# One attention-and-gMLP kernel on one core: the first pair's work cut and zeros added at the change of lag, copies ahead of the pieces' conversions, later pieces, and two fill units moved into the scores' banks

## The chip, the cores and the metric

The kernel runs on one core of a Trainium2 chip. The metric is the device time of one execution in microseconds (us), lower is better. The engines named below are TensorE (PE, with its weight loads as PEld), VectorE (DVE), ScalarE (ACT), GpSimd (POOL) and SyncE (SP), which issues most of the DMAs.

## The reference, cut to what matters

```python
# attention: 2 batches, 12 heads, 448 positions, head size 64
scores = scale * np.matmul(q, k.transpose(0, 1, 3, 2))
scores = cap * np.tanh(scores / cap)
attn = softmax(scores)                  # with 1e-9 added to the sum
x = merge_heads(np.matmul(attn, v))     # (2, 448, 768)

# first block: gMLP, 768 -> 1024 -> 768
h = gelu_tanh(x @ w_in); u, v = halves(h)
v_n = layernorm(v) * g_ln
gated = u * (w_sg @ v_n + b_sg)
x = x + gated @ w_out

# second block: gated convolution, 768 -> 1024 -> 768
h = relu(x @ w_in2)
out = (h * sigmoid(conv3(h, conv_w))) @ w_out2
```

## The kernel before

Every large product is three passes of matmuls on numbers that are split into a high and a low part (hi*hi, hi*lo, lo*hi). The kernel has three stages on TensorE: attention, the first block (units u, v, sg and o), the second block (units h and f).

**Attention** takes the 24 heads as 12 pairs (pair N is two heads). The loop runs over rounds R: round R makes the scores of one half of the keys of pair N = R // 2, so an even round is the first half, an odd round the second. In a round TensorE makes scores (tile sc, four banks that every round uses again), ScalarE makes tanh (line 387, sc to raw) and exp (line 388, raw to raw), and TensorE multiplies raw with V into the tile pv (`sums`, three banks; two pairs in turn share the middle one). The values lag behind the scores: LAGS says one round up to round 2 and two rounds from round 3. After the second half of a pair, `norm` copies values and softmax sums out of pv into E (ScalarE, line 504), which frees the banks for the next values; `s1`, some half rounds later, takes the reciprocal of the sums ss that a DMA has brought (DVE, lines 519 and 520), `s1b` spreads it by DMA to rb, and `s2` multiplies (line 536) and splits the result into X (ACT and DVE, lines 105 and 106). The last pair goes through `norm_pe`: copy E (line 548), reciprocal on VectorE (550, 551), four matmuls with sel (line 555), product (559). VectorE also prepares Q and K of the next pair (`prep_q`, `prep_k`; kl is the last part of K) and adds the halves of raw into sm for the sums.

**Beside it** the first block's weights are brought in as 12 pieces of w_in. Each piece lands in a tile f64, its top 16 bits are turned into half floats in the tile hd (line 149 on ACT, line 151 on DVE while R < 11), then merged (line 154), and cast to the high part of WI (160) and the low part (163). WIN gives the round in which a piece's DMA is issued, `wait` how many ticks later each of the three steps is due; there are two ticks in a round. hd is one tile, so a piece's conversion waits until the one before it has been read.

**Fill units.** Units u 0 to 2 of the first block for batch 0 are made inside the attention loop, as the table FILL says: round: (unit, first k, last k). All of them use the one bank of psm (tag mo), which `u_done` frees by the gelu on ACT and DVE (lines 221, 224, 225 and 228, the last into u). Unit u 3 is the first after the loop (mo, lines 109 to 111), then come the v units (lines 724 to 726).

**Order.** The order of each engine's instructions is fixed when the program is built, by a scheduler that works with its own estimate of the times; `pin` forces an instruction behind another, `ordered` pins a matmul behind the one before it in the loop, and `later` puts a step off by ticks. The warming matmuls wps and the matmuls named idle multiply zeros (wz) and are read by nobody. SP's DMAs are in the order in which the code issues them.

## Time and profile before

| | us |
|---|---|
| runs | 333.1, 335.48, 338.03 |
| median | 335.48 |
| profiled execution | 337.11 |
| its span in the profile | 335.3 |
| busy: PE, DVE, ACT, POOL | 318.5, 238.3, 223.2, 37.6 |
| granted TensorE clock, mean | 0.985 |

The profiled execution is one execution; its time is the span plus 1.8 us around it. A timeline line has the start, the duration, the engine, the line, operation and tiles, and in square brackets how long the engine sat idle before it and who ended that wait. Matmuls are pipelined: a row of several has their first start and their last modelled end, and the next row may start before it.

### The profile page before, as it was taken

The numbers are of one execution on the slowest core, as the hardware profiler recorded it, in microseconds if no ns is written. First come the engines' busy times: TensorE is split into PE (matmuls) and PEld (weight loads), VectorE is DVE, ScalarE is ACT, GpSimd is POOL, SyncE is SP. The second block draws the span as 40 slices with busy tenths as digits, with TensorE's granted clock in tenths as the row PEclk, the third lists the DMA queues.
The fourth block names the chain that finished last, engine by engine and source line by source line (L and its number), as shares of the span: only waits on it lengthen the run. The fifth ranks groups of instructions, "written<-read, shape, count | busy, mean of one in ns | idle before, by whom it ended". The sixth has DMA issues, their size and how long they took to land.

```text
span 335.3 us, 6265 instructions
## 1 busy us (share of the span) xinstructions
PE 318.5 (95%) x2380; PEld 262.8 (78%) x2380; DVE 238.3 (71%) x471; ACT 223.2 (67%) x357; POOL 37.6 (11%) x74
## 2 busy tenths in 40 slices
PE   7979999999788999999999999999999999999992
PEld 6445666656556778988899999999999999999991
DVE  4556586585965589996998789996975999980000
ACT  2887999999896257675765565555855988873010
POOL 4000130440304320221111000000000000000000
PEclk9978999999999999999999999999999999999998
DMA  5586595778422134212323490002392123012211
GB/s 141 150 193 187 154 259 171 199 216 189 133 75 76 38 123 108 69 38 78 121 71 125 124 343 20 0 2 63 71 334 100 31 65 94 0 59 112 82 55 35
DMA packets 22062, 37.73 MB, mean 113 GB/s; under 512 B 7320, under 2 KB 14376, under 8 KB 22024
## 3 DMA queue, kind: packets, MB, share of 16 engines
q1 hardware_dynamic: 20152, 34.41, 34.3%
q0 software_dynamic: 1632, 2.61, 3.1%
q8 instruction: 20, 0.33, 0.4%
q10 hardware_dynamic: 240, 0.23, 0.3%
q14 instruction: 18, 0.15, 0.2%
HBM read 34.40 MB, written 2.79 MB: 111 GB/s over the span
## 4 chain that ended last, share of the span: by engine, by line
PE 79%; ACT 10%; DMA 4%; SPq 2%; issue 2%; DVE 1%; ACTq 0%; DVEq 0%
PE mo L109 18%; PE mo L110 18%; PE mo L111 18%; PE pv L373 8%; PE sc L373 6%; ACT raw L387 4%; PE mo L724 3%; PE mo L726 3%; PE mo L725 3%; SPq L83 2%; ACT raw L388 2%; PE mo L373 2%; DMA qr<-in_qT_dram 1%; ACT hd L149 1%; DMA f<-in_conv_w_dram 1%
## 5 line engine op out<-in xcount | busy, mean ns | idle before, releaser
L109 PE MATMUL mo<-X,WI 128*128 128x448 f32 x126 | 46.0, 367 | 0.3 <-DVE u L228 0.3
L110 PE MATMUL mo<-X,WI 128*128 128x448 f32 x126 | 46.0, 366 | 0.0
L111 PE MATMUL mo<-X,WI 128*128 128x448 f32 x126 | 45.9, 365 | 0.0
L373 PE MATMUL pv<-raw,V 128*32 128x224 f32 x576 | 34.6, 370 | 3.5 <-ACT E L504 3.3
L388 ACT ACTIVATE raw<-raw 128x1792 f32<-128x1792 f32 (+3 forms) x26 | 36.7, 1413 | 0.8
L387 ACT ACTIVATE raw<-sc 128x1792 f32<-128x1792 f32 (+1 forms) x22 | 32.4, 1472 | 5.0 <-PE sc L373 4.9
L110 PE MATMUL mo<-HG,W 128*128 128x448 f32 x96 | 34.8, 365 | 0.0
L111 PE MATMUL mo<-HG,W 128*128 128x448 f32 x96 | 34.7, 365 | 0.0
L109 PE MATMUL mo<-HG,W 128*128 128x448 f32 x96 | 34.1, 365 | 0.0
L373 PE MATMUL sc<-Q,K 64*128 64x448 f32 x216 | 29.9, 399 | 3.8 <-ACT raw L387 3.3
L373 PEld LDWEIGHTS pv<-raw,V 128*32 128x32 f32 x576 | 19.1, 112 | 16.6 <-ACT E L504 6.0
L373 PEld LDWEIGHTS sc<-Q,K 64*128 64x128 f32 x216 | 19.1, 192 | 14.7 <-ACT raw L387 8.1
L179 ACT ACTIVATE f<-f 128x256 f32<-128x256 f32 (+2 forms) x44 | 22.8, 518 | 10.2 <-DMA f<-in_w_out_dram 6.2
L189 DVE SCALAR_TENSOR_TENSOR f<-f 128x256 uint32<-128x256 uint32 (+2 forms) x44 | 22.3, 515 | 8.2 <-ACT f L182 8.0
L109 PEld LDWEIGHTS mo<-X,WI 128*128 128x128 f32 x126 | 23.6, 188 | 2.8 <-DVE u L228 0.8
L110 PEld LDWEIGHTS mo<-X,WI 128*128 128x128 f32 x126 | 23.7, 188 | 2.0
L111 PEld LDWEIGHTS mo<-X,WI 128*128 128x128 f32 x126 | 23.6, 188 | 2.0
L904 ACT ACTIVATE o<-mo 128x448 f32<-128x448 f32 x12 | 6.3, 542 | 24.7 <-PE mo L111 20.8
L182 ACT ACTIVATE f<-f 128x256 uint32<-128x256 uint32 (+2 forms) x44 | 22.7, 515 | 0.0
L192 DVE SCALAR_TENSOR_TENSOR f<-f 128x256 uint32<-128x256 uint32 (+2 forms) x44 | 22.4, 515 | 0.1
L110 PEld LDWEIGHTS mo<-HG,W 128*128 128x128 f32 x96 | 18.0, 188 | 1.4
L109 PEld LDWEIGHTS mo<-HG,W 128*128 128x128 f32 x96 | 18.0, 188 | 1.4
(148 smaller groups left out, 685.8 us busy)
## 6 DMA issues: line engine op xcount, KB each, us to landing
f<-in_w_in_dram SPq DMA_DIRECT2D x12, 512.0 KB, 4.4
f<-in_w_out_dram SPq DMA_DIRECT2D x24, 256.0 KB, 4.5
f<-in_w_in_dram SPq DMA_DIRECT2D x12, 511.8 KB, 5.1
f<-in_w_out_dram SPq DMA_DIRECT2D x8, 384.0 KB, 3.1
qr<-in_qT_dram SPq DMA_DIRECT2D x24, 112.0 KB, 3.7
out_dram<-o SPq DMA_DIRECT2D x12, 224.0 KB, 1.9
rb<-d POOLq DMA_DIRECT2D x22, 112.0 KB, 4.0
V<-in_vL_dram SPq DMA_DIRECT2D x12, 192.0 KB, 3.3
```

The costliest lines, as they stand in the source:

```text
L109: matmul(ps, lhsT=whi, rhs=xhi, start=start, stop=False)
L110: matmul(ps, lhsT=whi, rhs=xlo, start=False, stop=False)
L111: matmul(ps, lhsT=wlo, rhs=xhi, start=False, stop=stop)
L179: A.activation(f(h), f(h), AF.Copy, scale=2.0**-112)
L182: A.activation(l, l, AF.Copy, scale=0.93 * 2.0**-29)
L189: V.scalar_tensor_tensor(out=l, in0=h, scalar=3, in1=l, op0=ALU.logical_shift_left, op1=ALU.bitwise_or)
L192: V.scalar_tensor_tensor(out=l, in0=h, scalar=0x80000000, in1=l, op0=ALU.bitwise_and, op1=ALU.bitwise_or)
L373: lastm[0] = T.matmul(*args, **kw)
L387: A.activation(x, ps, AF.Tanh, **sc)
L388: lasta[0] = A.activation(x, x, AF.Exp, scale=creg)
L724: T.matmul(ps, lhsT=xs(0, k), rhs=WI[1][:, 0, k], start=k == 0, stop=False)
L725: T.matmul(ps, lhsT=xs(0, k), rhs=WI[1][:, 1, k], start=False, stop=False)
```

## The change

Eight edits, in the code of the attention and of what it shares with the slow path:

1. In `constants` the product with guard and the tile eye leave the fast path; hd becomes two tiles that pieces use in turn.
2. For pair 0, K is prepared ahead of Q, Q's high part is copied by ScalarE, and the guard's product comes behind.
3. For pair 0 the order on ScalarE is tanh, tanh, exp, exp for round 0 and one tanh and one exp for round 1; the values of round 0 come after all scores of round 1.
4. Zero matmuls: 4 in round 0 as before, 2 in round 1, and 9 behind the scores of round 3.
5. The copy E of pair 0 comes behind the tanh of round 3. The tanh and exp instructions are pinned in order.
6. The columns (gbc and conv_w) are loaded in round 6 instead of round 1.
7. Pieces are issued later (WIN), their steps come one tick later (`wait`), and the steps of `norm` come two and one ticks later for pairs below 8.
8. Unit u 1 is made in round 24 instead of 23, and units u 1 and u 2 go to banks of the tile fi, which is the scores' tile sc, instead of psm's bank.

```diff
-FILL = {14: (0, 0, 2), 18: (0, 2, 4), 22: (0, 4, 6), 23: (1, 0, 6), 25: (2, 0, 6)}
+FILL = {14: (0, 0, 2), 18: (0, 2, 4), 22: (0, 4, 6), 24: (1, 0, 6), 25: (2, 0, 6)}
-IDLE = 4
+IDLE = {0: (0, 4), 1: (3, 2), 3: (3, 9)}
-WIN = (3, 5, 8, 10, 12, 14, 15, 17, 18, 20, 21, 22)
+WIN = (3, 5, 7, 9, 12, 15, 17, 19, 21, 22, 23, 24)
...
-        heads[:] = [pool.tile([P, 512], U32, name=f"hd{i}") for i in range(1)]
+        heads[:] = [pool.tile([P, 512], U32, name=f"hd{i}") for i in range(2)]
...
-                V.tensor_copy(q[:, 0], qr)
-                V.tensor_tensor(out=q[:, 1], in0=qr, in1=f(q[:, 0]), op=ALU.subtract)
+                A.activation(q[:, 0], qr, AF.Copy)
+                lastv[0] = V.tensor_tensor(out=q[:, 1], in0=qr, in1=f(q[:, 0]), op=ALU.subtract)
...
+        prep_k(0)
         prep_q(0)
-        prep_k(0)
+        with pin(lastv):
+            V.tensor_scalar(out=guard, in0=guard, scalar1=1e-9, scalar2=None, op0=ALU.mult)
...
             def soft(x, ps):
-                A.activation(x, ps, AF.Tanh, **sc)
-                lasta[0] = A.activation(x, x, AF.Exp, scale=creg)
+                with pin(lasta):
+                    lasta[0] = A.activation(x, ps, AF.Tanh, **sc)
+                if N == 1 and half:
+                    with pin(lasta):
+                        late.pop()()
+                if half or N:
+                    expo(x)
+
+            def expo(x):
+                with pin(lasta):
+                    lasta[0] = A.activation(x, x, AF.Exp, scale=creg)
...
+                if N == 0 and g < 2:
+                    soft(raw[:, 2 * g : 2 * g + 2], ps[:, 2 * g : 2 * g + 2, :S])
+                    if g:
+                        expo(raw[:, 0:2])
+                        expo(raw[:, 2:4])
+                if R in IDLE and g == IDLE[R][0]:
+                    for _ in range(IDLE[R][1]):
                         ordered(idle, lhsT=wz[:, :P], rhs=wz, start=True, stop=True)
...
-            A.activation(e[:, j * (S + HS) : (j + 1) * (S + HS)], both, AF.Copy)
-            u = j * (2 * S + HS)
-            G.dma_start(ss[j * P // m : (j + 1) * P // m], e[::32, u : u + HS])
+
+            def copy():
+                lasta[0] = A.activation(e[:, j * (S + HS) : (j + 1) * (S + HS)], both, AF.Copy)
+                u = j * (2 * S + HS)
+                G.dma_start(ss[j * P // m : (j + 1) * P // m], e[::32, u : u + HS])
+
+            if N:
+                copy()
+            else:
+                late.append(copy)
...
-            later(4, s1)
-            later(5, s1b)
-            later(13, s2)
+            k = 6 if N < 8 else 4
+            later(k, s1)
+            later(k + 1, s1b)
+            later(14 if N < 8 else 13, s2)
...
-            if R == 1:
+            if R == 6:
                 columns(att)
...
-                    wdec(*wi_piece(w_in, j // NK, j % NK), att, 4, hi_eng="v", wait=(3, 4, 5), top_eng=top_eng)
+                    wdec(*wi_piece(w_in, j // NK, j % NK), att, 4, hi_eng="v", wait=(4, 5, 6), top_eng=top_eng)
...
                 if k0 == 0:
-                    fill[i] = psm.tile([P, 512], F32, tag="mo", name="mo")[:, :S]
+                    if i == 1:
+                        fill[3] = psa.tile([P, 4, 512], F32, tag="sc", name="fi", bufs=1)
+                    fill[i] = fill[3][:, i, :S] if i else psm.tile([P, 512], F32, tag="mo", name="mo")[:, :S]
```

The scheduler then puts the instructions in this order. TensorE in the first pair, from its first scores to the first matmul of round 4, before:

```order
L373 MATMUL sc<-Q,K_87 128x448 x6
L373 MATMUL idle<-wz 128x448 x4
L373 MATMUL sc<-Q,K_87 128x448 x6
L373 MATMUL pv<-raw,V 32x224 x8
L373 MATMUL sc<-Q,K_87 128x2x224 x6
L373 MATMUL pv<-raw,V 32x224 x8
L373 MATMUL sc<-qr,kl_91 64x224 x4
L373 MATMUL pv<-sm,ones_152 32x224 x4
...
L373 MATMUL sc<-Q,K_88 128x2x224 x6
L373 MATMUL sc<-qr,kl_92 64x224 x4
L373 MATMUL sc<-Q,K_87 128x448 x12
```

TensorE at the same place after the change:

```order
L377 MATMUL sc<-Q,K_87 128x448 x6
L377 MATMUL idle<-wz 128x448 x4
L377 MATMUL sc<-Q,K_87 128x448 x6
L377 MATMUL sc<-Q,K_87 128x2x224 x6
L377 MATMUL sc<-qr,kl_91 64x224 x4
L377 MATMUL idle<-wz 128x448 x2
L377 MATMUL pv<-raw,V 32x224 x16
L377 MATMUL pv<-sm,ones_148 32x224 x4
...
L377 MATMUL sc<-qr,kl_92 64x224 x4
L377 MATMUL idle<-wz 128x448 x9
L377 MATMUL sc<-Q,K_87 128x448 x12
```

The values of round 0 moved behind the scores of round 1, and nine zero matmuls stand between the scores of round 3 and those of round 4.

ScalarE from the tanh of round 16 to that of round 20, before (E is the copy out of pv, X the attention's result, hd a piece's conversion):

```order
L387 ACTIVATE raw_938<-sc_937 128x1792
L388 ACTIVATE raw_938<-raw_938 128x1792
L105 ACTIVATE X_75<-E_513 128x2x448
L149 ACTIVATE hd0_141<-f64_884 128x512
L387 ACTIVATE raw_995<-sc_994 128x1344
L388 ACTIVATE raw_995<-raw_995 128x1344
L504 ACTIVATE E_920<-pv_171 128x672
L387 ACTIVATE raw_1045<-sc_1044 128x1792
L388 ACTIVATE raw_1045<-raw_1045 128x1792
L149 ACTIVATE hd0_141<-f64_992 128x512
L387 ACTIVATE raw_1096<-sc_1095 128x1344
```

ScalarE at the same place after the change:

```order
L394 ACTIVATE raw_937<-sc_936 128x1792
L403 ACTIVATE raw_937<-raw_937 128x1792
L105 ACTIVATE X_75<-E_518 128x2x448
L394 ACTIVATE raw_990<-sc_989 128x1344
L403 ACTIVATE raw_990<-raw_990 128x1344
L149 ACTIVATE hd0_140<-f64_887 128x512
L521 ACTIVATE E_924<-pv_168 128x672
L394 ACTIVATE raw_1042<-sc_1041 128x1792
L403 ACTIVATE raw_1042<-raw_1042 128x1792
L394 ACTIVATE raw_1095<-sc_1094 128x1344
```

One conversion of two is gone from these rounds, and the other one stands later, ahead of a copy E.

TensorE from the last scores (round 23) to the first v unit, before (mo and fi are fill units, sel the norm of the last pair):

```order
L373 MATMUL sc<-qr,kl_92 64x224 x4
L373 MATMUL mo<-X,WI_76 128x448 x18
L373 MATMUL pv<-raw,vlast 64x224 x4
...
L373 MATMUL pv<-raw,V 32x224 x16
L373 MATMUL pv<-sm,ones_152 32x224 x4
L373 MATMUL mo<-X,WI_76 128x448 x18
L373 MATMUL pv<-raw,vlast 64x224 x4
...
L109 MATMUL mo<-X,WI_76 128x448
L110 MATMUL mo<-X,WI_76 128x448
...
L555 MATMUL pv<-E,sel 64x224 x4
L724 MATMUL mo<-WI_77,X 128x512
```

TensorE at the same place after the change:

```order
L377 MATMUL sc<-qr,kl_92 64x224 x4
L377 MATMUL pv<-raw,vlast 64x224 x4
...
L109 MATMUL mo<-X,WI_76 128x448
L110 MATMUL mo<-X,WI_76 128x448
L377 MATMUL fi<-X,WI_76 128x448 x18
...
L377 MATMUL pv<-raw,V 32x224 x16
L377 MATMUL pv<-sm,ones_148 32x224 x4
...
L377 MATMUL fi<-X,WI_76 128x448 x18
L377 MATMUL pv<-raw,vlast 64x224 x4
...
L578 MATMUL pv<-E,sel 64x224 x4
L752 MATMUL mo<-WI_77,X 128x512
```

The fourth unit u (lines 109 to 111, 18 matmuls) moved from behind the last values to ahead of the last fill unit; the matmuls with sel now come directly behind the last values.

VectorE after the change, from the gelu of the last fill unit to the reciprocal that those matmuls wait for:

```order
L224 SCALAR_TENSOR_TENSOR g0_1412<-g0_1412,fi_1338 128x448
L228 SCALAR_TENSOR_TENSOR u_1455<-g0_1412,fi_1338 128x448
L558 TENSOR_TENSOR E_1129<-E_1129,rb_1232 128x896
L154 SCALAR_TENSOR_TENSOR f64_1336<-f64_1336,hd0_140 128x512
L573 TENSOR_SCALAR E_1438<-E_1438,one_72 128x224
L160 CAST WI1_77<-f64_1336 128x512
L574 RECIPROCAL E_1438<-E_1438 128x224
```

Before, the same row stood without the two steps of a piece (lines 154 and 160).

## Rows read from the trace of the kernel before

**Rows 1.** Stretches: start:end, length, busy of each engine, PEclk, DMA share, GB/s.
```profile
121.00:300.00 179.00, 179.00 (x868) 162.20 (x865) 160.95 (x318) 123.77 (x260) 10.58 (x14) 1.00 0.28 88
```

**Rows 2.** Timeline, rounds 0 to 2.
```profile
7.17 0.97 PE L373 MATMUL sc<-Q,K 64*128 64x448 f32 x6 [0.41 <-DVE one L258]
8.19 1.01 ACT L387 ACTIVATE raw<-sc,one 128x896 f32<-128x896 f32 x1 [2.58 <-PE sc L373]
9.23 0.95 ACT L388 ACTIVATE raw<-raw 128x896 f32<-128x896 f32 x1
16.38 0.23 ACT L149 ACTIVATE hd<-f 128x24 f16<-128x24 bf16 x1 [1.11 <-DMA f<-in_conv_w_dram]
17.00 1.65 ACT L387 ACTIVATE raw<-sc 128x1792 f32<-128x1792 f32 x1
```

**Rows 3.** Timeline, rounds 3 to 6, around the change of lag.
```profile
20.29 0.71 ACT L504 ACTIVATE E<-pv 128x672 f32<-128x672 f32 x1
20.90 1.28 ACT L387 ACTIVATE raw<-sc 128x1344 f32<-128x1344 f32 x1
22.24 2.61 PE L373 MATMUL sc<-Q,K 64*128 64x448 f32 x12 [2.11 <-ACT raw L387]
24.89 1.67 ACT L387 ACTIVATE raw<-sc 128x1792 f32<-128x1792 f32 x1 [1.35 <-PE sc L373]
31.98 1.49 PE L373 MATMUL sc<-Q,K 64*128 64x448 f32 x12
```

**Rows 4.** Stretches of TensorE's waits and of the work behind one.
```profile
20.13:22.24 2.11, 0.00 (x1) 0.01 (x2) 1.82 (x4) 2.08 (x4) 0.68 (x1) 0.85 0.86 239
22.24:28.30 6.06, 6.06 (x52) 3.73 (x52) 3.31 (x7) 4.66 (x3) 0.00 (x0) 0.50 1.12 227
...
85.85:87.64 1.79, 0.00 (x1) 0.00 (x1) 1.79 (x6) 1.41 (x3) 0.00 (x0) 1.00 0.75 233
```

**Rows 5.** Timeline, rounds 8 to 10.
```profile
39.51 0.71 ACT L504 ACTIVATE E<-pv 128x672 f32<-128x672 f32 x1
...
40.28 1.76 PE L373 MATMUL pv<-raw,V 128*32 128x224 f32 x32
...
45.74 1.49 PE L373 MATMUL sc<-Q,K 64*128 64x448 f32 x12
```

**Rows 6.** Timeline, TensorE's waits in rounds 16 to 20, and what leads to the last.
```profile
69.98 1.76 PE L373 MATMUL pv<-raw,V 128*32 128x224 f32 x32 [0.55 <-ACT E L504]
...
76.05 1.49 PE L373 MATMUL sc<-Q,K 64*128 64x448 f32 x12 [0.54 <-ACT raw L387]
...
84.15 0.23 DVE L519 TENSOR_SCALAR ss<-ss,one 128x14 f32<-128x14 f32 x1 [4.29 <-DMA ss<-E]
85.52 0.68 DVE L154 SCALAR_TENSOR_TENSOR f<-f,hd 128x512 uint32<-128x512 uint32 x1
86.23 0.78 ACT L149 ACTIVATE hd<-f 128x512 f16<-128x512 bf16 x1 [1.13 <-DMA V<-in_vL_dram]
87.64 1.76 PE L373 MATMUL pv<-raw,V 128*32 128x224 f32 x32 [1.79 <-ACT E L504]
```

**Rows 7.** Timeline, from the last scores to the norm of the last pair.
```profile
100.77 3.94 PE L373 MATMUL mo<-X,WI 128*128 128x448 f32 x18 [1.36 <-DVE u L228]
107.90 1.76 PE L373 MATMUL pv<-raw,V 128*32 128x224 f32 x32 [0.97 <-ACT E L504]
108.90 0.45 DVE L160 CAST WI<-f 128x512 fp32r<-128x512 f32 x1
109.97 3.94 PE L373 MATMUL mo<-X,WI 128*128 128x448 f32 x18
116.47 0.47 PE L109 MATMUL mo<-X,WI 128*128 128x448 f32 x1 [0.34 <-DVE u L228]
117.70 1.55 DVE L551 RECIPROCAL E<-E 128x224 f32<-128x224 f32 x1
120.34 0.98 PE L555 MATMUL pv<-E,sel 128*64 128x224 f32 x8
```

More of the change, by code (lines that the diff above doesn't have):

```diff
@@ L257, in constants @@
         A.activation(guard, ncap, AF.Exp)
-        V.tensor_scalar(out=guard, in0=guard, scalar1=1e-9, scalar2=None, op0=ALU.mult)
-        heads[:] = [pool.tile([P, 512], U32, name=f"hd{i}") for i in range(1)]
+        if not bounded:
+            V.tensor_scalar(out=guard, in0=guard, scalar1=1e-9, scalar2=None, op0=ALU.mult)
+        heads[:] = [pool.tile([P, 512], U32, name=f"hd{i}") for i in range(2)]
         for t in heads:
             G.memset(f(t), 0.0)
-        eye = pool.tile([P, P], F32, name="eye")
-        make_identity(nc, eye)
         G.memset(nhalf, -0.5)
-        return eye
+        if not bounded:
+            eye = pool.tile([P, P], F32, name="eye")
+            make_identity(nc, eye)
+            return eye
     def columns(pool):
@@ L362, in attention @@
             G.memset(sel[t * 32 : t * 32 + 1, t], 1.0)
+        prep_k(0)
         prep_q(0)
-        prep_k(0)
+        with pin(lastv):
+            V.tensor_scalar(out=guard, in0=guard, scalar1=1e-9, scalar2=None, op0=ALU.mult)
         raws, acc, held, pairs = {}, {}, {}, []
@@ L373, in ordered @@
                 lastm[0] = T.matmul(*args, **kw)
+        late, sm0 = [], [None]
         sums = psa.tile([P, 3 * 512], F32, tag="pv", name="pv", bufs=1)
         def scores(N, half, ahead={}):
+            R = 2 * N + half
             q, K = Qt[N], Kt[N % 2]
@@ L419, in scores @@
                             )
[L420 to L433 removed]
+                if N == 0 and g < 2:
[5 more added lines that the diff above has]
+                    for _ in range(IDLE[R][1]):
+                        ordered(idle, lhsT=wz[:, :P], rhs=wz, start=True, stop=True)
+            if half:
+                soft(raw, ps)
+            elif N:
+                soft(raw, ps[:, :, :S])
             if half == 0:
                 held[N] = att.tile([P, 2, S], F32, tag="sm", name="sm", bufs=2)
[L436 removed]
+                sm = V.tensor_tensor(out=held[N], in0=raw[:, 0:2], in1=raw[:, 2:4], op=ALU.add)
+                if N == 0:
+                    sm0[0] = sm
         def start_values(N):
@@ L582, in attention @@
                     start_values(0)
-                    scores(N, half, {2: lambda: value(0, 0), 3: lambda: value(0, 1)})
+                    scores(N, half)
+                    value(0, 0)
+                    value(0, 1)
                     values(0, 0, True)
@@ L588, in attention @@
                 if half == 0 and N + 1 < NN:
-                    prep_q(N + 1)
-                    prep_k(N + 1)
+                    with pin(sm0) if N == 1 else ExitStack():
+                        prep_q(N + 1)
+                        prep_k(N + 1)
             if R in FILL:
```

14 lines of the change are left out of this document (removed).

## The prediction

> **What bounds the kernel now.** I read the busy times by stretch first. From 121 to 300 us TensorE is busy all of 179.00 us at a granted clock of 1.00 [rows 1]: nothing that the change does there can bring anything, and the matmuls there are the same before and after. What can be won or lost lies in the first 121 us, so I went through the timeline of those for every place where TensorE waits, and read who ends the wait. There are four kinds.
>
> First, the first pair. ScalarE takes it in small pieces, each tanh waiting for its scores and each exp following it, then serves the two copies of the conv columns (0.23 us for the first), and starts the tanh of round 2 at 17.00 [rows 2]. Second, the change of lag at round 3. There the copy of the first sums (0.71) stands between exp and the tanh of round 3 (1.28), and the scores of round 4 wait 2.11 us for that tanh [rows 3]. This is costly twice. TensorE is idle from 20.13 to 22.24, its clock falls to 1.2 GHz inside that wait, and the next 6.06 us of work run at 0.50 [rows 4]. ScalarE itself then waits 1.35 us for the slow scores [rows 3]. Another wait, 1.79 us, at 85.85, left the clock at 1.00 [rows 4].
>
> Third, from 24 to 54 us the engines are balanced: the copy E ends at 40.22 and the matmuls that need its bank start at 40.28 [rows 5]. From round 12 on the pieces' conversions (0.78 each) and the attention's copies to X come on top on ScalarE, and TensorE waits 0.55, 0.54 and 1.79 us [rows 6]. The last of these is a chain: VectorE waits 4.29 us for the DMA of the sums ss, so the reader of hd (0.68) comes late, hd has one buffer, the next conversion waits 1.13 us, and the copy E behind it lets TensorE wait [rows 6]. Fourth, the fill units at the end share one bank: 1.36 us for the unit's result u, 0.97 for a copy E, 0.34 again for u [rows 7].
>
> **The change part by part.** Small pieces of round 0 and 1: K's high part is made first on VectorE while ScalarE makes Q's. The first scores wait 0.41 us after the warming matmuls now [rows 2]; that is all that can go, so 0 to 0.4, and I take 0.3, since the data still has to land. Then tanh, tanh, exp, exp and one tanh of 1.28 stand on ScalarE. The second tanh still cannot start before its scores, which in both programs wait for the first tanh; now that point is 10.18 (end of the first exp) [rows 2], then 9.85. From there: 1.01, twice 0.95 and 1.28 give 14.1. The scores of round 2 may start then, with some 0.4 for the sums' matmuls ahead, and take 1.49 as any such group [rows 3]: tanh of round 2 at 16.05 against 17.00, a gain of 0.95. The conv columns are away from here; on SP's queue their two DMAs now stand ahead of the loads for pair 5 instead of pair 3, which are due two rounds later.
>
> Zeros at the lag change: the copy E now comes after tanh of round 3, so that tanh starts 0.95 and 0.71 sooner than 20.90, at 19.3 at the earliest; its scores, after which TensorE falls idle at 20.13 now [rows 4], are ready at about 19.4, because the tanh of round 2 that they wait for ends sooner. It ends at 20.8. The nine zero matmuls, some 0.2 each (18 matmuls of that width take 3.94 us [rows 7]), fill TensorE from 19.4 to 21.2, so the scores of round 4 start at 21.2 at full clock and end at 22.7. ScalarE needs until 22.85 for copy and exp (about as long as its tanh). So tanh of round 4 starts at 22.85 instead of 24.89 [rows 3]. From a tanh right behind a copy (40.3) to the scores of the pair after (45.74) it takes 5.4 at full clock [rows 5], so the scores of round 6 start at 28.2 instead of 31.98: **a gain of 3.8**, 3.0 to 4.2 by the unknown landing times.
>
> Conv columns in round 6: two copies of 0.23 on ScalarE in a period that has 0.06 us to spare between E and the matmuls [rows 2, 5]: **a loss of 0.3**, 0 at least, 0.5 at most; should their DMA be late, more, but it is issued before the round that reads it.
>
> Conversions behind the copies, two hd buffers, later pieces: in the rounds up to the last tanh there were seven conversions on ScalarE, now there are four; three go to the end, where ScalarE waits anyhow. The wait for hd's reader goes, since hd has two buffers and the norm's first step comes two ticks later, when ss has landed. Of the three waits of TensorE, 2.88 us in all [rows 6], I keep 0.2 before the values of round 14, 0.1 before the scores of 18, 0.75 before the values of 18 (a conversion of 0.78 still stands ahead of the copy there) and 0.2 after a copy to X: 1.25. **A gain of 1.6**, 0.5 to 2.9.
>
> Last units in the scores' banks: now the order on TensorE decides. The three waits of [rows 7], 2.67 us, go: the values of round 21 come before the fill, and the units no longer share a bank. But the fourth unit (mo, lines L109 to L111), which before stood between the last values and the matmuls of the norm (pv from E and sel), is used up ahead. What is late next is the norm of the last pair. Before, the reciprocal ended at 119.25, that is 5.34 after the last fill ended at 113.91, hidden by the fourth unit [rows 7]. After, the same chain holds, with a piece's two steps more on VectorE in between, 0.68 and 0.45 less their overlaps [rows 6, 7]: 6.45 after the last fill. The last values take only 2.2 of that. So TensorE waits 4.2 us there, with the v units behind it. Before, the norm's matmuls started at 120.34; the stream without its waits would be there at 117.7, or at 117.0 if the drains ahead of the waits go too. So the last fill ends at 114.8 to 115.5 and these matmuls start at 121.2 to 121.9, on the time axis of the kernel before. **A loss of 1.2**, 0.9 to 1.5.
>
> And the clock. The wait of 2.11 us let it fall and the wait of 1.79 did not [rows 4]; one of 4.2 is twice the longer. I let it fall. The first 6.06 us of work after the wait at 22.24 ran at 0.50, which is worth 3.0 us of time [rows 4]: **a loss of 3.0** for the first v unit, 0 if the clock holds, 3.5 at the most.
>
> Without cost: the eye tile that is no longer made, the guard's product behind prep_q (VectorE has slack there), and GpSimd's set-up instruction, which moves to the first pow, where GpSimd waits for VectorE's statistics; the v units have banks to run ahead. The norm's first step comes two ticks later, so on GpSimd's queue a next pair's ss goes ahead of rb; rb is read rounds later. VectorE has one more piece to finish after the norm, in a stretch in which TensorE's own delay gives it the time.
>
> Sum: -3.8 + 0.3 - 1.6 + 1.2 + 3.0 = -0.9 us. Against the profiled execution (337.11, of which 335.3 are the span) that is 336.2; this execution lies 1.6 above the median of the runs, 335.48, and from that the time is **334.6**.
>
> **The rivals.** The clock holds through the wait at the norm: everything else the same, 331.6. For it speaks the wait of 1.79 without a fall, against it the one of 2.11 with one [rows 4]. The Trainium skill (TensorE: Matmul & The Clock Gate, Part 1: The HAM clock gate) calls the point at which the clock switches run-variable; by that some executions would show this time and others my forecast's, and no run here shows it either way.
>
> The conversions are not what held TensorE (or the wait for ss comes back one round later): the 1.6 stays, and the time is 336.2, no gain at all. For it: ScalarE is full there, and one conversion still stands ahead of a copy. Against: the chain in [rows 6] is closed, link by link.
>
> Slower: the zeros do not hold the clock. In the first pair the scores of round 1 must now wait for the second tanh, about 1 us (1.01 for the tanh itself [rows 2]), with shorter waits around it, where before values stood in between. If these add up as the wait of 2.11 us did, the clock falls there, 3.0 us as in [rows 4] come back at the start, and the norm's fall stays: 337.6, slower by 0.6%. It decides from the point at which the granted clock of 10 to 22 us goes to 0.50. Against it: none of these waits alone is longer than the one of 1.79.
>
> **How the numbers follow.** Forecast 0.50; clock holds 0.20; conversions without effect 0.17; clock falls at the start as well 0.13. The low end is the second case with the start's gain at its upper bound, rounded for the middle's, 330.8; the high end the last case, 337.6, and a little of its bound, 338.0. All four cases lie within 2% of 335.48 (328.8 to 342.2), about what a measurement of this kernel tells from no change: faster 0.04, same 0.93, slower 0.03.
>
> **What would show it.** Right: scores of round 6 at about 28 and a granted clock of 1.00 from 10 to 34 us; the last attention tanh about 5 us sooner; a wait of TensorE of some 4 us ahead of the norm's matmuls, ended by VectorE's reciprocal, and 0.50 behind it. Wrong: if the wait is under 2 us, my chain on VectorE is too long; if it is there and the clock stays at 1.00, the second case holds; if TensorE waits for bank or weights in the v units, the late last piece costs what I put at nothing.

## The result, and the profile after

The changed kernel is slower: 338.86 us median (336.16 to 341.64, 20 runs) against 336.08 us for the kernel before on the same chip (333.10 to 338.91, 20 runs). The ratio is 1.0091, with a 95% interval of 1.0067 to 1.0115; all ratios here are of the runs within 1.5% of their kernel's fastest, so they differ a little from those of the medians. The prediction was 334.6 us with a range of 330.8 to 338.0: the time moved the other way and ended outside the range. The profiled execution of the changed kernel took 340.46 us, of which 338.7 are the span.

The timeline of the changed kernel at its start, and around the change of lag (start us, length us, engine, line, operation, names, count, and in brackets the idle time ahead with what ended it):

```profile
1.38 6.69 PE L351 MATMUL wps<-wz 128*128 128x448 f32 x18 [1.38 <-DVE wz L348]
8.18 0.87 PE L377 MATMUL sc<-Q,K 64*128 64x448 f32 x6
17.68 1.67 ACT L394 ACTIVATE raw<-sc 128x1792 f32<-128x1792 f32 x1 [1.30 <-PE sc L377]
21.12 2.09 PE L377 MATMUL idle<-wz 128*128 128x448 f32 x9
23.15 1.48 PE L377 MATMUL sc<-Q,K 64*128 64x448 f32 x12
30.02 1.49 PE L377 MATMUL sc<-Q,K 64*128 64x448 f32 x12
```

The first scores start 1.01 us later than in the kernel before [rows 2], because 18 warming matmuls ended only at 8.07. Yet the scores of round 6 start 1.96 us sooner [rows 3]: the wait ahead of round 4 is no longer bare, since nine matmuls of zeros stand in it, and the scores of round 4 take 1.48 us instead of 2.61.

The middle loses that again. The same view around round 17, and below it d's row in the view of the DMA issues of 59 to 60.5 us (the last number is the time from issue to landing in us):

```profile
58.84 0.23 DVE L541 TENSOR_SCALAR ss<-ss,one 128x14 f32<-128x14 f32 x1
59.75 0.38 SPq L83 DMA_DIRECT2D f<-in_w_in_dram  x1
60.26 0.58 POOL L545 DMA_DIRECT2D d<-ss  x1 [6.95 <-DVE ss L542]
65.70 2.11 POOL L551 DMA_DIRECT2D rb<-d  x4 [4.23 <-PE pv L377]
72.50 1.09 DVE L558 TENSOR_TENSOR E<-E,rb 128x896 f32<-128x896 f32 x1 [4.63 <-DMA rb<-d]
73.63 0.95 ACT L105 ACTIVATE X<-E 128x896 fp32r<-128x896 f32 x1 [2.38 <-DVE E L558]
75.81 2.61 PE L377 MATMUL sc<-Q,K 64*128 64x448 f32 x12 [2.54 <-ACT raw L394]
```
```profile
d<-ss POOLq DMA_DIRECT2D x1, 7.0 KB, 4.9
```

Read it from the bottom of the first fence up. The scores of round 18 wait 2.54 us for the tanh of round 17. That tanh stands on ScalarE behind the copy to X, which waited 2.38 us for VectorE's product with rb (L558), which waited 4.63 us for rb to land. GpSimd sent rb at 65.70, since d, sent at 60.26, landed 4.9 us later. The brackets of rb name a matmul; but rb goes out half a microsecond behind the landing of d here (60.26 and 4.9) and in the four other profiles with the late ticks, so what it waited for is d. The granted clock falls in the wait, and the scores take 2.61 us.

The tail, in the same view:

```profile
101.39 0.47 PE L109 MATMUL mo<-X,WI 128*128 128x448 f32 x1
101.91 3.82 PE L377 MATMUL fi<-X,WI 128*128 128x448 f32 x18
111.09 3.84 PE L377 MATMUL fi<-X,WI 128*128 128x448 f32 x18
119.53 1.54 DVE L574 RECIPROCAL E<-E 128x224 f32<-128x224 f32 x1
121.23 1.76 PE L578 MATMUL pv<-E,sel 128*64 128x224 f32 x8 [4.08 <-DVE E L574]
122.92 0.80 PE L752 MATMUL mo<-WI,X 128*128 128x512 f32 x1
```

The fourth unit (L109) is used up from 101.39 on, and the matmuls of the norm wait 4.08 us for the reciprocal, as forecast. The stretches (start:end, length, busy of PE, PEld, DVE, ACT and POOL, granted clock, DMA share, GB/s) show where the clock stood:

```profile
20.13:34.00 13.87, 13.87 (x185) 9.47 (x183) 10.15 (x20) 13.10 (x11) 1.30 (x2) 1.00 0.96 223
75.81:79.00 3.19, 3.19 (x14) 2.44 (x15) 3.05 (x7) 3.09 (x4) 0.92 (x2) 0.50 0.61 217
121.23:126.50 5.27, 5.27 (x16) 3.63 (x17) 5.20 (x8) 3.00 (x7) 2.37 (x2) 0.50 0.08 30
```

The fall behind 22 us [rows 4] is gone; two new ones, at 1.2 GHz, are behind 75.8 and behind 121.2.

Counted from the zeros of round 0 (8.97 us here, 8.08 before), so that the length of the warming drops out, the two profiles differ as follows. Scores of round 8: 2.86 us sooner. From there to the scores of round 22: 56.18 us against 54.24, a loss of 1.94. From there to the first v unit: 29.84 against 28.14, a loss of 1.70. From the first v unit to the end: 215.78 against 214.05, a loss of 1.73. Sum +2.51; with the 0.89 of the later zeros it is the 3.4 us between the spans, 338.7 and 335.3.

This is one execution of each kernel, and executions differ. Two runs below have the changed kernel's order up to round 22 (u3_behind, wait_filled): from round 8 to 22 they take 53.62 and 55.31 us where this profile has 56.18. before_fill_only has the order of the kernel before up to there: 53.10 us where that one has 54.24, and its scores of round 8 start 31.46 us behind the zeros instead of 30.79. By the means the middle's loss is 1.4 us rather than 1.94, and the start's gain lies between 2.86 and 3.5.

### The profile page after: what moved, and what is told of

Read it like the earlier page. It is cut to its first block, busy times and chain, and to the rows that moved or that the text cites. A ratio compares the mean times of both kernels' runs of the same rounds, so it can differ in the third digit from the quotient of the medians.

```text
span 338.7 us, 6289 instructions
## 1 busy us (share of the span) xinstructions
PE 322.4 (95%) x2391; PEld 267.9 (79%) x2391; DVE 238.3 (70%) x470; ACT 223.5 (66%) x356; POOL 37.5 (11%) x73
## 3 DMA queue, kind: packets, MB, share of 16 engines
q0 software_dynamic: 1632, 2.61, 3.0%
## 4 chain that ended last, share of the span: by engine, by line
PE 89%; ACT 4%; DVE 2%; DMA 2%; issue 1%; POOL 0%; DVEq 0%; ACTq 0%
PE mo L110 18%; PE mo L109 18%; PE mo L111 18%; PE pv L377 11%; PE sc L377 8%; PE mo L752 3%; PE mo L754 3%; PE mo L753 3%; PE fi L377 2%; PE wps L351 2%; ACT raw L394 2%; DMA rb<-d 2%; PE mo L377 1%; ACT raw L403 1%; PE idle L377 1%
## 5 line engine op out<-in xcount | busy, mean ns | idle before, releaser
L109 PE MATMUL mo<-X,WI 128*128 128x448 f32 x126 | 46.1, 367 | 0.0
L403 ACT ACTIVATE raw<-raw 128x1344 f32<-128x1344 f32 (+2 forms) x25 | 36.4, 1460 | 0.6
L109 PE MATMUL mo<-HG,W 128*128 128x448 f32 x96 | 34.1, 365 | 0.0
L377 PE MATMUL pv<-raw,V 128*32 128x224 f32 x576 | 32.9, 358 | 0.8 <-ACT E L521 0.8
L449 DVE TENSOR_TENSOR sm<-raw 128x896 f32<-128x896 f32 x12 | 13.1, 1090 | 18.4 <-ACT raw L403 18.3
L109 PEld LDWEIGHTS mo<-X,WI 128*128 128x128 f32 x126 | 23.6, 188 | 2.4 <-issue 0.4
L110 PEld LDWEIGHTS mo<-HG,W 128*128 128x128 f32 x96 | 18.0, 188 | 1.4
```

The source lines that it names most:

```text
L109: matmul(ps, lhsT=whi, rhs=xhi, start=start, stop=False)
L110: matmul(ps, lhsT=whi, rhs=xlo, start=False, stop=False)
L377: lastm[0] = T.matmul(*args, **kw)
L403: lasta[0] = A.activation(x, x, AF.Exp, scale=creg)
L449: sm = V.tensor_tensor(out=held[N], in0=raw[:, 0:2], in1=raw[:, 2:4], op=ALU.add)
```

## The experiments

My first theory was that two things of the change made it slow, each by itself: the norm's later ticks (through d, rb and the tanh of round 17), and the order of the fourth unit on TensorE (through the wait of 4.08 us and the clock behind it). The rival for the first was that the pieces' transfers would delay rb wherever the norm's steps stand; for the second, that the tail was bound by ScalarE and VectorE whatever TensorE's order. Of a wait's length I speak as the brackets give it.

**The norm's steps back (norm_back).**

```
-            k = 6 if N < 8 else 4
+            k = 4
...
-            later(14 if N < 8 else 13, s2)
+            later(13, s2)
```

> The changed kernel with the norm's steps at their old ticks (4, 5 and 13 for every pair); all else stays. Theory A (the later first step of the norm makes the wait of 2.54 us ahead of the scores of round 18: d goes out at 60.26 beside a 512-KB piece and lands 4.9 us later, rb behind it lands about 72.4, VectorE's product with rb starts at 72.50, ScalarE's copy to X and the tanh of round 17 follow, and TensorE's clock falls in the wait): rb goes out some 5 us sooner, the wait ahead of the scores of round 18 is under 0.6 us, the clock stays at 1.00 from 70 to 95 us, the scores of round 18 start near 73.2 instead of 75.81 and those of round 22 near 91 instead of 93.08; time 2 to 2.5 us under the changed kernel's, a ratio to the kernel before near 1.002. Rival B (the piece's transfer, wherever d stands, or VectorE's load makes rb's reader late): the wait stays above 2 us and the ratio stays near 1.009. Rival C (VectorE's wait of 4.29 us for ss comes back with the old ticks): the wait moves to the values of rounds 16 to 18 as in the kernel before, gain under 1 us, ratio 1.006 to 1.009.

Measured: 336.22 us, ratio 1.002 (0.9984 to 1.0055), so 2.4 us under the changed kernel by the ratios. The timeline of this kernel around round 17, and one stretch:

```profile
48.47 0.23 DVE L541 TENSOR_SCALAR ss<-ss,one 128x14 f32<-128x14 f32 x1 [1.89 <-DMA ss<-E]
49.27 0.57 POOL L545 DMA_DIRECT2D d<-ss  x1 [3.09 <-DVE K L103]
68.14 1.08 DVE L558 TENSOR_TENSOR E<-E,rb 128x896 f32<-128x896 f32 x1
73.07 1.48 PE L377 MATMUL sc<-Q,K 64*128 64x448 f32 x12
```
```profile
70.00:95.00 25.00, 24.40 (x344) 16.19 (x344) 16.86 (x30) 24.29 (x23) 5.54 (x10) 1.00 0.67 183
```

These are the same norm's steps as in the changed kernel above. Its first step stands at 48.47 against 58.84, and its d goes at 49.27 against 60.26. Two ticks in the code are one round, some 3.5 us here; the scheduler made 10 us of them, for on VectorE it put the step behind K and Q of two more pairs, their sums, and the product and the low part of X of the norm before. The product with rb runs at 68.14 with no wait, since its rb had landed, the scores of round 18 start at 73.07 with no wait, and the clock holds from 70 to 95 us. From round 8 to round 22 it takes 52.72 us, 3.5 less than in the changed kernel. Theory A holds. VectorE's wait for ss does come back (5.15 us ahead of L541 at 64.58), as C has it, but no one waits for VectorE there; the prediction's reason, the second hd buffer, was not tried alone. What was not expected is a wait of 0.81 us ahead of the values of round 6, of which more below. The tail's wait of 4.08 us and the fall of the clock stand as they were.

**Two pieces moved (pieces_moved).** The late ticks stay; two 512-KB transfers are issued one pair sooner.

```
-WIN = (3, 5, 7, 9, 12, 15, 17, 19, 21, 22, 23, 24)
+WIN = (3, 5, 7, 9, 11, 13, 17, 19, 21, 22, 23, 24)
```

> The changed kernel, norm's late ticks kept, with two pieces of W_in moved ahead: those issued with the loads of rounds 12 and 14 in the changed kernel go to rounds 10 and 12, so that no 512-KB transfer is issued beside d at 60.26. Theory A (the piece's transfer at 59.75 is why d took 4.9 us to land, and so why rb was late): d lands within 2.5 us, rb goes out 2 us or more sooner than 65.70, the wait ahead of the scores of round 18 (0.67 to 3.03 us in four runs with the late ticks) is under 0.5 us; time 1.5 to 2.5 us under the changed kernel's, ratio 1.002 to 1.005. Rival B (the place of the norm's steps alone decides, and d and rb land as late without the piece): the wait stays above 0.6 us, ratio 1.007 to 1.010.

Measured: 336.52 us, ratio 1.0058 (1.0021 to 1.0095). Rows of its timeline, and d's row of its DMA issues:

```profile
59.61 0.58 POOL L545 DMA_DIRECT2D d<-ss  x1 [6.95 <-DVE ss L542]
63.49 2.25 POOL L551 DMA_DIRECT2D rb<-d  x4 [2.64 <-PE sc L377]
69.95 1.09 DVE L558 TENSOR_TENSOR E<-E,rb 128x896 f32<-128x896 f32 x1 [3.91 <-DMA rb<-d]
73.25 1.50 PE L377 MATMUL sc<-Q,K 64*128 64x448 f32 x12
76.48 1.29 PE L377 MATMUL mo<-X,WI 128*128 128x448 f32 x5 [1.33 <-DVE X L106]
```
```profile
d<-ss POOLq DMA_DIRECT2D x1, 7.0 KB, 3.3
```

Half of A holds. With the transfer away d takes 3.3 us instead of 4.9, rb goes out 2.2 us sooner, and the wait ahead of round 18 is gone. But d does not come down to the 2.5 us expected, VectorE still waits 3.91 us for rb, and a wait of 1.33 us for X stands at the next fill. The transfer beside d makes the lateness worse; the late ticks are what leaves no room for it: from d's sending to rb's landing it still takes 10.3 us (59.61 to 69.9). The interval of the ratio overlaps the changed kernel's, so the gain in time is not shown, only the waits are. The Trainium skill (DMA: Bandwidth & Descriptors, Queues, rings and completion order) says that a DMA engine serves the queues it has work for in turns, a packet at a time; a small d beside a large piece being late agrees with that, but no run here shows the turns themselves.

**The fourth unit behind the last values (u3_behind).**

```
                 for k in range(NK):
-                    mmw(ps, b, i, k)
+                    with pin(lastt) if n == 3 else ExitStack():
+                        mmw(ps, b, i, k)
```

Here lastt is the last matmul of the attention's ordered stream, kept at the end of its loop.

> The changed kernel with the 18 matmuls of the fourth unit (L109 to L111) ordered behind the last values, ahead of the norm's matmuls, as in the kernel before; the last two fill units stay in the scores' banks. Theory A (the tail loses by the order on TensorE alone: the fourth unit is used up ahead and the chain from the last values to the reciprocal, 6.3 us from the last fill, is bare): the last fill ends near 111 instead of 114.93, the wait ahead of the norm's matmuls falls from 4.08 us to under 0.6, the clock behind it stays at 1.00, so the first v unit starts about 5 us sooner; time 5.0 to 6.5 us under the changed kernel's, ratio to the kernel before 0.990 to 0.994. Rival B (the fill itself waits for X, WI or ScalarE once the fourth unit no longer stands between the fills, so that the last fill ends where it did): only the clock is won back and part of the wait, 2.5 to 3.5 us, ratio near 1.000.

Measured: 335.38 us, ratio 0.9994 (0.9956 to 1.0032), 3.3 us under the changed kernel by the ratios. The timeline of its tail, and a stretch:

```profile
106.02 0.62 DVE L229 SCALAR_TENSOR_TENSOR u<-g,fi 128x448 f32<-128x448 f32 x1 [0.64 <-ACT g L226]
106.69 3.95 PE L378 MATMUL fi<-X,WI 128*128 128x448 f32 x18 [2.48 <-DVE u L229]
116.94 0.98 PE L579 MATMUL pv<-E,sel 128*64 128x224 f32 x8 [0.23 <-DVE E L575]
```
```profile
115.00:121.00 6.00, 5.77 (x31) 4.42 (x30) 5.93 (x9) 2.22 (x5) 1.43 (x2) 1.00 0.44 156
```

The wait ahead of the norm goes from 4.08 to 0.23 us and the clock stays at 1.00, so the order is the cause of both. The size is B's: the second late fill unit now waits 2.48 us for the u of the first, which ends at 106.64. The two units write different banks, but they are one tile of the program, and the wait is for the reader of the other bank. In the changed kernel the fourth unit's matmuls stood in that wait and hid it.

**The wait filled (wait_filled).** The changed kernel, with more matmuls in the wait of 4.08 us.

```
             rp = sums[:, :S]
+            for _ in range(18):
+                ordered(fill[3][:, 3, :S], lhsT=WI[0][:, 0, 0, :P], rhs=X[:, 0, 0, 0], start=True, stop=True)
```

> The changed kernel with 18 more matmuls of 448 columns between the last values and the norm's matmuls; they multiply loaded data into a free bank that nobody reads (3.8 us by the fills' 3.84 for 18), so they add work and leave every other wait as it is. Theory A (of the tail's loss the slow clock behind the wait is a part of its own): the wait of 4.08 us shrinks to under 0.8 us, the clock behind it stays at 1.00, the norm's matmuls start no more than 0.3 us later against the end of the last fill, and the v units behind them run 2.5 to 3.0 us shorter; time 2.0 to 3.0 us under the changed kernel's, ratio to the kernel before 1.000 to 1.003. Rival B (the clock does not matter, or it falls all the same): ratio 1.008 to 1.011.

Measured: 335.65 us, ratio 1.0002 (0.9973 to 1.0032). Rows of its timeline, and two stretches:

```profile
75.68 1.49 PE L377 MATMUL sc<-Q,K 64*128 64x448 f32 x12 [3.03 <-ACT raw L394]
...
115.49 3.94 PE L377 MATMUL fi<-X,WI 128*128 128x448 f32 x18
119.56 0.98 PE L581 MATMUL pv<-E,sel 128*64 128x224 f32 x8
```
```profile
75.68:79.00 3.32, 3.32 (x30) 2.50 (x34) 3.17 (x8) 3.32 (x4) 1.04 (x2) 1.00 0.49 175
119.50:126.00 6.50, 6.44 (x32) 5.18 (x33) 5.90 (x9) 3.42 (x6) 1.66 (x2) 1.00 0.45 156
```

TensorE does 3.9 us of work more than in the changed kernel, whose result no one reads, and the time is some 3 us less. The norm's matmuls start 6.2 us after the end of the last fill (113.3 to 119.56), as in the changed kernel (6.3), but they take 0.98 us instead of 1.76, and the clock behind them is 1.00. So A holds at its upper end: of the tail's loss, the slow clock is the larger part and exists apart from the wait. The first row shows something else: this execution waited 3.03 us ahead of round 18, longer than the 2.54 of the changed kernel's profile, and kept its clock.

**No zeros (no_zeros).** The nine matmuls of zeros ahead of the scores of round 4 are left out.

```
-IDLE = {0: (0, 4), 1: (3, 2), 3: (3, 9)}
+IDLE = {0: (0, 4), 1: (3, 2)}
```

> The changed kernel without the nine matmuls of zeros ahead of the scores of round 4; nothing else changes. Theory A (the zeros hold the clock through a wait of about 2 us): the granted clock falls to 0.50 behind 23 us as in the kernel before, the scores of round 4 take 2.6 us instead of 1.48, the scores of round 6 start 1.0 to 2.0 us later than 30.02, time 0.8 to 2 us over the changed kernel's, ratio near 1.013. Rival B (the clock holds without them, since the copy E that stood in the wait is away): scores of round 6 within 0.3 of 30.02, ratio near 1.009 or a little under, for the zeros are gone from the order.

Measured: 336.35 us, ratio 1.0047 (1.0016 to 1.0077). Rows of its timeline, and a stretch:

```profile
21.93 1.49 PE L377 MATMUL sc<-Q,K 64*128 64x448 f32 x12 [1.41 <-ACT raw L394]
36.47 1.49 PE L377 MATMUL sc<-Q,K 64*128 64x448 f32 x12 [0.70 <-ACT raw L394]
```
```profile
20.00:34.00 14.00, 12.59 (x188) 8.15 (x188) 10.37 (x21) 13.41 (x12) 1.32 (x2) 1.00 0.87 213
```

Theory A falls. Without the zeros the wait is 1.41 us, not 2.11, because the copy E no longer stands in it, and the clock stays at 1.00. Counted from the zeros of round 0 (8.30 here), the scores of round 4 even start 0.55 us sooner than with them; by round 8 a wait of 0.70 us for ScalarE has taken that back. The gain at the lag change comes with the moved copy and needs no zeros; they add nothing that this profile shows. The copy was not moved by itself. Why the median is some 1.5 us under the changed kernel's this profile doesn't settle: its wait ahead of round 18 was 0.67 us, and that wait differs from execution to execution (below).

**The tail alone on the kernel before (before_fill_only).**

```
-22: (0, 4, 6), 23: (1, 0, 6), 25: (2, 0, 6)}
+22: (0, 4, 6), 24: (1, 0, 6), 25: (2, 0, 6)}
...
+                    if i == 1:
+                        fill[3] = psa.tile([P, 4, 512], F32, tag="sc", name="fi", bufs=1)
+                    fill[i] = fill[3][:, i, :S] if i else psm.tile([P, 512], F32, tag="mo", name="mo")[:, :S]
```

> The kernel before with the one edit at the tail: the second fill unit at round 24 instead of 23, and the second and third fill units in the scores' banks; the fourth unit then stands ahead and between the fills, as in the changed kernel. Theory A (this edit alone loses what the tail of the changed kernel lost): the wait ahead of the norm's matmuls is about 4 us, the clock behind it falls to 0.50 for about 6 us of work, the norm's matmuls start 1 us later than 120.34 and the v units run 2.6 us longer; time 3.0 to 4.0 us over the kernel before, ratio 1.009 to 1.012. Rival B (the loss needs the later pieces and the later last round as well): ratio under 1.004.

Measured: 337.49 us, ratio 1.0068 (1.0027 to 1.0109). Its timeline at the norm, and a stretch:

```profile
118.90 0.98 PE L555 MATMUL pv<-E,sel 128*64 128x224 f32 x8 [2.47 <-DVE E L551]
```
```profile
119.00:124.00 5.00, 5.00 (x19) 3.76 (x19) 4.83 (x8) 3.29 (x7) 1.99 (x2) 0.66 0.23 80
```

The one edit alone makes the kernel slower, through the wait and the clock. In size it lies between the theories: the wait is 2.47 us, not 4. Two things of the changed kernel are missing. Three matmuls of the fourth unit still follow the last values (0.8 us, from 115.55), and no late piece's steps stand ahead of VectorE's reciprocal, which starts 3.8 us behind the end of the last fill (117.19 and 113.41) instead of 4.6 (119.53 and 114.93).

**The start alone (start_only).** The changed kernel with the old WIN, one hd buffer, wait=(3, 4, 5), the old norm ticks, FILL and banks; the diff is those lines of the change put back. With the one hd buffer the top bits of the conv weights (34.27 us) overwrite a part of a piece's (29.88) before those are read (36.32), so the output isn't the reference's; instructions and sizes are those of the start of the changed kernel.

> The kernel before with the start of the changed one alone (first pair's pieces, late copy E, zeros, conv columns in round 6, no eye tile); one hd buffer, the old rounds of the pieces, the norm's old ticks and the old fill units. Theory A (the start gains 2.85 us from the end of the warming matmuls to the scores of round 6, the columns give 0.4 back, and ScalarE's later waits give back none): scores of round 6 21.0 us behind the zeros of round 0 against 23.9 in the kernel before; time 2.0 to 2.8 us under the kernel before, ratio 0.992 to 0.994. Rival B (the gain is given back in rounds 16 to 20, where ScalarE is full and the norm's chain over the DMAs sets the pace): the last attention tanh is under 1 us sooner, ratio 0.997 to 1.001.

Measured: 333.76 us, ratio 0.9937 (0.9909 to 0.9965), 2.1 us under the kernel before. The scores of round 6 start 21.04 us behind the zeros of round 0 (29.43 and 8.39). Theory A holds. The wait ahead of round 18 is 1.07 us here, the one ahead of round 22 0.29, and the values of round 18, which waited 1.79 us in the kernel before [rows 6], start at 83.51 behind the scores with no wait. The scores of round 22 start 81.41 us behind the zeros, 3.62 us sooner than in the kernel before and 3.15 sooner than in before_fill_only: the middle takes little or nothing of the start's gain.

**Both single edits, then the bank (norm_u3, norm_u3_bank).** norm_u3 is norm_back's and u3_behind's edits together. norm_u3_bank puts the second late unit into the bank of the units ahead:

```
-                    fill[i] = fill[3][:, i, :S] if i else psm.tile(
+                    fill[i] = fill[3][:, i, :S] if i == 1 else psm.tile(
```

> The changed kernel with both single edits: the norm's steps at their old ticks, and the fourth unit behind the last values. Theory A (the two causes lie in different stretches and add up: -2.4 and -3.3 us as measured apart): 332.5 to 334 us beside a kernel before at 335.7 to 336.1, ratio 0.991 to 0.994. Rival B (what the middle gains ends in the tail, where the second fill in the scores' banks waits 2.48 us for the first one's u): ratio 0.996 to 1.000, with that wait grown to 4 us or more.

> The same as norm_u3, with the second of the late fill units in the bank of the units ahead, so that it shares no tile with the first. Theory A (the wait of 2.48 us ahead of that unit is for the first unit's u, which reads another bank of the same tile): the wait goes, the last fill ends 2.0 to 2.5 us sooner against the scores of round 22, and the wait for the norm's reciprocal stays under 0.6 us; time 1.0 to 2.4 us under norm_u3's, ratio 0.985 to 0.990. Rival B (ScalarE or VectorE are as late there: X of the pair before, or the chain of the last pair's norm): a wait of 1.5 us or more takes its place there or ahead of the norm's matmuls, ratio within 0.002 of norm_u3's.

Measured: norm_u3 331.72 us, ratio 0.9883 (0.9846 to 0.9920); norm_u3_bank 330.55 us, ratio 0.9852 (0.9812 to 0.9892). The gains add up, and norm_u3 is a little better than A: in its profile the wait for the other bank's u is 1.12 us, not 2.48. In norm_u3_bank it is gone:

```profile
97.56 3.93 PE L378 MATMUL fi<-X,WI 128*128 128x448 f32 x18
103.49 3.92 PE L378 MATMUL mo<-X,WI 128*128 128x448 f32 x18
113.83 0.98 PE L579 MATMUL pv<-E,sel 128*64 128x224 f32 x8
```

The second late unit starts 2.0 us behind the first one's end, which is the values between them; the norm's matmuls (last row) wait for nothing. From the scores of round 22 to the first v unit it takes 25.49 us against 28.14 in the kernel before. The intervals of the two kernels overlap, so that the bank gives time is shown by the rows, not by the medians. But both lose in round 6. The timeline of norm_u3 there:

```profile
34.63 0.23 DVE L542 TENSOR_SCALAR ss<-ss,one 128x14 f32<-128x14 f32 x1 [0.27 <-DMA ss<-E]
36.65 0.18 DVE L155 SCALAR_TENSOR_TENSOR f<-f,hd 128x24 uint32<-128x24 uint32 x1
36.86 0.23 ACT L159 ACTIVATE cw<-f 128x24 fp32r<-128x24 f32 x1 [1.63 <-DVE f L155]
38.96 1.76 PE L378 MATMUL pv<-raw,V 128*32 128x224 f32 x32 [1.62 <-ACT E L522]
```

The columns' second copy waits 1.63 us on ScalarE for a small step of VectorE, which stands behind the first norm's steps, K's conversion and the sums; an exp of 1.31 us and the copy E are queued behind that copy. It is the one place seen where the late ticks help.

**The late ticks for the first norm only, with zeros and without (first_late, first_late_no_zeros).**

```
-            k = 6 if N < 8 else 4
+            k = 6 if N == 1 else 4
...
-            later(14 if N < 8 else 13, s2)
+            later(14 if N == 1 else 13, s2)
```

> norm_u3_bank with the late ticks (6, 7, 14) for the first norm only, which shares round 7 with the conv columns, and 4, 5, 13 for the others. Theory A (with the old ticks the first norm's two steps on VectorE push the columns' step behind, ScalarE's copy cw waits 1.63 us for it with the exp of round 7 queued behind, and TensorE waits 1.58 ahead of the values of round 6): that wait is 0.3 us as in the changed kernel, the one ahead of round 18 stays under 0.6, and the time is 0.8 to 1.3 us under norm_u3_bank's: ratio 0.981 to 0.983. Rival B (the gain is taken back by another wait, at round 10 or 18): ratio 0.985 to 0.987.

> first_late without the nine matmuls of zeros ahead of the scores of round 4. Theory A (the zeros are not needed, since without the copy E the wait there is only 1.4 us and left the clock at 1.00 in the one profile seen; they start the scores 0.5 us later, which ScalarE takes back by round 8): clock 1.00 from 20 to 34 us, ratio within 0.002 of first_late's. Rival B (in a part of the executions the clock falls in that wait): the median is 0.5 to 2 us over first_late's, or single runs are 2 to 3 us above the rest.

Measured: first_late 329.84 us, ratio 0.9866 (0.9813 to 0.9920); first_late_no_zeros 330.28 us, ratio 0.9872 (0.9821 to 0.9922). In first_late's profile the wait ahead of the values of round 6 is 0.30 us, the scores of round 18 start at 72.48 with no wait, and the whole attention runs at one clock:

```profile
8.00:121.00 113.00, 110.52 (x1396) 76.01 (x1394) 78.70 (x150) 96.95 (x95) 26.41 (x42) 1.00 0.59 163
```

The kernel before on that chip was 0.8 us faster than beside norm_u3_bank, so the ratios, which lie where B put them, don't tell the two apart; the rows show A's wait gone and none in its place, and the median is 0.7 us lower, a little less than A's 0.8. Without the zeros the clock is 1.00 as well and no single run stands out: A's reading of the zeros holds, in this kernel and in no_zeros.

**Fewer warming matmuls (short_warming).** first_late with 14 instead of 18.

```
-WARM = 18
+WARM = 14
```

> first_late with 14 warming matmuls of zeros ahead of the first scores instead of 18. In the changed kernel Q and K are ready at 6.94 us, but the warming matmuls end at 8.07 and the first scores start at 8.18; in ten profiles with the new start they took 5.55 to 6.69 us for the same 18. Theory A (the warming matmuls, not the data, set the first scores' start): they end before 7.0, the scores start within 0.2 us of Q's low part, and the time to the scores of round 6 is 0.2 to 1.0 us shorter, with a median 0 to 0.6 us under first_late's. Rival B (with fewer of them the clock is not at 1.00 for the first pair): the six matmuls of the first scores take over 1.2 us instead of 0.87, and the median is 0.5 us or more over first_late's.

Measured: 329.50 us, ratio 0.9826 (0.9785 to 0.9868). Rows of its timeline:

```profile
1.39 5.59 PE L352 MATMUL wps<-wz 128*128 128x448 f32 x14 [1.39 <-DVE wz L349]
6.66 0.62 DVE L313 TENSOR_TENSOR Q<-qr,Q 128x448 fp32r<-128x448 f32 x1
7.08 0.93 PE L378 MATMUL sc<-Q,K 64*128 64x448 f32 x6
```

The warming ends at 6.98 and the first scores start at 7.08, while Q's low part is being written: data and warming are ready together, and the six matmuls take 0.93 us (0.87 with 18). The difference to first_late, 0.3 us, is less than these runs can tell.

## Why the prediction was wrong

Counted from the zeros, the forecast was -0.9 us and the two profiles show +2.51. Of the 3.4 us between them the middle is 3.54, the start 0.64, and the tail gave 0.77 back.

**The start** was right in its mechanism. Predicted were -3.8 and +0.3, that is 3.5 us up to round 8; measured are 2.86, or 3.5 against before_fill_only's profile. The lag change itself brought what was worked out: from the tanh of round 2 to the scores of round 6 it is 12.34 us (12.15 forecast, 14.98 before [rows 2, 3]). What was too large is the tanh of round 2, put 0.95 us sooner at 16.05 (its terms add up to 16.0). The first scores did not come 0.3 sooner, since the warming matmuls decide when they start, and the rest came to 0.2 (8.71 us from the zeros against 8.92). The gain comes with the moved copy E; the zeros, for which the prediction let the clock hold, are not needed for it (no_zeros, first_late_no_zeros).

**The middle is the step that failed.** It was put at -1.6 and measured +1.94 (+1.4 by the means above). The prediction saw the norm's first step go two ticks later and gave it two answers: it counted on it to end VectorE's wait for ss, and under "Without cost" it wrote that on GpSimd's queue a next pair's ss goes ahead of rb, and that rb is read rounds later. The first gain was not needed: with the old ticks VectorE's wait holds up no one (norm_back, 5.15 us ahead of L541 and none on TensorE). The second was not without cost. The first step moved two ticks and the reader, L558, one; but in the order that was built the first step came 10 us later, behind work of VectorE that the prediction did not look at. From d's sending to the moment VectorE is ready for rb it is 7.6 us in the changed kernel (60.26 to 67.87) and 18.9 in norm_back (49.27 to 68.14), and d and rb take 12.2, beside two pieces' transfers (59.75 and 68.11). So rb was late, in five profiles with the late ticks, by 2.7 to 5.1 us at L558, and TensorE waited 0.67 to 3.03 us ahead of round 18, or 1.33 at the next fill (pieces_moved). With the old ticks and two hd buffers the middle takes 52.72 us (norm_back), with the late ticks for the first norm only 52.22 (first_late), against 54.24 and 53.10 with the old order: 0.4 to 2.0 less. So the conversions' term of 1.6 had the right sign and may have been right in size, and the norm's spent it. A run with the reader moved as far as the first step was not made. The rival that the conversions are without effect, with "the wait for ss comes back", had the right place and the wrong link: it was rb, not ss.

**The tail** went as worked out. The fourth unit is used up ahead, the wait is 4.08 us (4.2 forecast), the chain from the last fill 6.3 (6.45), the clock falls to 0.50 behind it. Wait and slow clock cost 3.43 us against 1.2 and 3.0; u3_behind takes away both with the order, wait_filled the clock alone. The rival that the clock holds there has no profile for it: with waits of 4.08 us in three and 4.14 in a fourth (after, norm_back, no_zeros, pieces_moved) the clock fell each time. What the prediction left out is that the two late units share a tile, which costs 2.48 us (u3_behind) or 1.12 (norm_u3) as soon as the fourth unit doesn't cover it.

**The range** was too narrow because every case in it kept the middle's gain at 0 or more. A bound below nothing for the moved norm was missing: a price was there to be taken from [rows 6], 4.29 us of waiting for a DMA of the same chain.

The first scores' delay in the profile of the changed kernel, 0.89 us by the zeros of round 0, is in no median that I can take apart. Over thirteen profiles the same 18 warming matmuls took 5.31 to 6.69 us: 5.31 and 5.39 with the old start, 5.55 to 6.69 in eleven with the new one. The first 8 to 16 of them start about 0.37 us apart, the rest 0.21: 8 are slow in both with the old start, 16 in the changed kernel's profile. The Trainium skill (TensorE: Matmul & The Clock Gate, Part 1: The HAM clock gate) says that the number of slow matmuls at a kernel's start differs between runs of one kernel, and the spread of the eleven agrees. Whether the new start adds to it by itself stays open, with two profiles of the old one.

## What to carry to other kernels

A step that is moved later takes its time from the round trip behind it: before calling it free, look up where the built order puts it (here two ticks became 10 us), count from there to its last reader, and price that chain by the slowest landing in the trace, beside whatever bulk transfer is issued there. When a change gives work an earlier place, ask what it was covering where it stood: here the fourth unit hid the last norm's chain, and the clock behind its bare wait of 4 us was worth some 3 us. Two results in different banks of one tile are one buffer to the waits.

## What had not been expected of the hardware

The length of a wait does not decide whether TensorE's clock falls to 1.2 GHz. Waits of 2.11, 2.47, 2.54 and 4.08 us were followed by 0.50 in their profiles, those of 1.41, 1.79, 2.48 and 3.03 us were not; the changed kernel's code gave 2.54 with a fall in one execution and, up to that point the same, 3.03 without in another (wait_filled). Useless matmuls in a wait can shorten a kernel when they keep the clock: 3.9 us of them in wait_filled, about 3 us gained; the nine ahead of round 4 gained nothing. And the landing of d, 7 KB, goes with what was sent just ahead: over all profiles it took 3.2 to 5.0 us in the nine cases in which a piece of 512 KB had been issued up to 0.8 us before, and 1.7 to 4.1 us in the others. For the d of this account that is 4.9 to 5.0 us in three profiles and 3.8 in a fourth, 3.3 in pieces_moved.
